# Seven products of halves for both weight products, in two stages, on one Trainium2 core

## The chip, the core and the metric

The program runs on one core of one Trainium2 chip. Five engines work on their own instruction streams and wait for each other through semaphores: TensorE (PE in the profile, with PEld its loads of the stationary operand), VectorE (DVE), ScalarE (ACT), GpSimd (POOL) and SyncE (SP), which issues nearly all DMAs. The metric is the device time of one execution in microseconds.

## The reference

```python
rms = np.sqrt(np.mean(x * x, axis=-1, keepdims=True) + 1e-06)      # q and k, each row of 64
q_n, k_n = (rmsnorm(q, g_q), rmsnorm(k, g_k))
scores = scale * np.matmul(q_n, k_n.transpose(0, 1, 3, 2))
attn = np.exp(scores - np.max(scores, axis=-1, keepdims=True))
attn = attn / (np.sum(attn, axis=-1, keepdims=True) + 1e-09)
x = np.matmul(attn, v)              # then (B,H,S,D) -> (B*S, H*D)
h = x @ w_in
g = h * (1.0 / (1.0 + np.exp(-h)))
return (g @ w_out).astype(np.float32)
```

There are 8 batches of 12 heads, 448 positions and 64 features, so x is 3584 x 768; w_in is 768 x 2048, w_out 2048 x 768. The weights come as float64 and are rounded on the chip to float32; everything is computed in float32.

## The kernel before

`bounded` (L268) is the function that runs. It takes the heads in 48 pairs, n = 0 to 47, six pairs a batch. For a pair, `normalise` (L281) squares q and k on ScalarE, reduces on VectorE, and takes the power and the two products on GpSimd; `transpose` (L309) turns q and k on TensorE, and ScalarE or VectorE copies the result out of PSUM; `scores` (L325) makes four blocks of scores and ScalarE their exponentials (L336); `weigh` (L338) multiplies them with v; `add_up` (L353) sums the exponentials on VectorE for the denominator; `divide` (L372) spreads the sums over the partitions with a matmul against ones (L379), takes the reciprocal (L383) and writes xT, a 128 x 448 tile of x transposed.

Six such tiles hold a batch. `feed_forward(b)` (L390 on) is a generator that yields after every matmul: 16 blocks f of 128 hidden features, each the sum of six matmuls of 448 columns (L400), with the activation on ScalarE out of PSUM (L408); then the product with w_out, in tiles of 128 tokens and two halves of 384 columns, 16 matmuls each (L416), copied out by VectorE (L422) and stored. A batch has 448 = 3.5 x 128 tokens, so the half tile of two batches is put together in g_joint. The hidden activations never leave the chip.

The order of everything is written out by hand: instructions stand on each engine in the order in which the program calls them. `begin` starts the feed-forward of batch b - 1 during batch b, and `fill()` (L437) is called four times a pair and emits as many matmuls as are due, evenly over the pairs. Batch 0 has nothing to fill with, and the feed-forward of batch 7 follows after the last pair. All matmuls of the feed-forward share two PSUM banks (`mm`, bufs=2).

The weights stay in SBUF. `Weights.load` (L80) brings a piece in as int64 on the SP queue, `split` (L96) takes it apart on ScalarE, `round` (L116) finishes it with three VectorE instructions and a GpSimd addition (L134 to L145). There are 24 pieces of w_in and 32 of w_out; six are rounded in batch 0 and fifty in batch 1:

```python
rounds = [0, 0, 0, 1] if b == 0 else [2, 3, 2, 3]
```

Lines of the trace name tiles: sc scores, e exponentials, es their sums, av the product with v, tr transposes and the spread sums, mm the feed-forward.

## Time and profile before

| what | value |
|---|---|
| time, median of 3 runs (lowest, highest) | 1670.94 us (1665.33, 1671.11) |
| time of the profiled execution | 1668.44 us |
| its span | 1666.6 us |
| mean granted TensorE clock | 0.986 |
| DMA traffic | 70.22 MB |
| matmuls of w_in, L400 | 1536 instructions, 604.3 us busy |
| matmuls of w_out, L416 | 1536 + 256 instructions, 517.9 + 86.8 us busy |

A float32 matmul of the program shows as two MATMUL and two LDWEIGHTS instructions. In the page's list of groups a row reads: line, engine, operation, output<-inputs, shapes, count | busy us, mean ns of one | idle time of the engine ahead of it and what ended it. In a timeline a row reads: start us, length us, engine, line, operation, and in brackets the idle time before it with its releaser.

### The profile page before, as it was taken

The numbers are of one execution on the slowest core, as the hardware profiler recorded it, in microseconds if no ns is written. First come the engines' busy times: TensorE is split into PE (matmuls) and PEld (weight loads), VectorE is DVE, ScalarE is ACT, GpSimd is POOL, SyncE is SP. The second block draws the span as 40 slices with busy tenths as digits, with TensorE's granted clock in tenths as the row PEclk, the third lists the DMA queues.
The fourth block names the chain that finished last, engine by engine and source line by source line (L and its number), as shares of the span: only waits on it lengthen the run. The fifth ranks groups of instructions, "written<-read, shape, count | busy, mean of one in ns | idle before, by whom it ended". The sixth has DMA issues, their size and how long they took to land.

```text
span 1666.6 us, 14205 instructions
## 1 busy us (share of the span) xinstructions
PE 1599.6 (96%) x5440; PEld 789.0 (47%) x5440; DVE 561.4 (34%) x660; ACT 516.9 (31%) x840; POOL 307.0 (18%) x208
## 2 busy tenths in 40 slices
PE   5887797999999999999999999999999999999998
PEld 1233343444555444544455444554455444555555
DVE  4898556422224223322322232242222422320000
ACT  4565544233212343133311343223321234211100
POOL 4555334111111121121111211211121112100000
PEclk9899999999999999999999999999999999999999
DMA  6352344100111000110011100110001100000000
GB/s 205 93 152 69 100 111 124 43 17 22 26 31 42 22 18 26 28 53 17 6 36 31 49 17 6 48 42 23 17 26 31 42 23 17 11 15 5 1 19 20
DMA packets 51984, 70.22 MB, mean 42 GB/s; under 512 B 5316, under 2 KB 44740, under 8 KB 51908
## 3 DMA queue, kind: packets, MB, share of 16 engines
q1 hardware_dynamic: 51584, 69.23, 14.5%
q8 instruction: 45, 0.74, 0.2%
q14 instruction: 31, 0.25, 0.0%
q10 hardware_dynamic: 324, 0.00, 0.0%
HBM read 58.20 MB, written 11.01 MB: 42 GB/s over the span
## 4 chain that ended last, share of the span: by engine, by line
PE 83%; DVE 2%; issue 1%; POOL 1%; ACT 1%; POOLq 0%
PE mm L416 33%; PE mm L400 32%; PE sc L331 8%; PE av L345 7%; PE tr L379 2%; PE tr L317 2%; POOL W L145 0%; DVE r L383 0%; DVE W L141 0%; DVE es L363 0%; DVE W L137 0%; DVE W L134 0%; ACT W L113 0%; ACT last L112 0%; DVE es L358 0%
## 5 line engine op out<-in xcount | busy, mean ns | idle before, releaser
L400 PE MATMUL mm<-xT,W 128*128 128x448 f32 x1536 | 604.3, 547 | 22.1 <-ACT g_joint L408 18.4
L416 PE MATMUL mm<-W,g_own 128*128 128x384 f32 x1536 | 517.9, 493 | 9.3 <-POOL W L145 6.9
L400 PEld LDWEIGHTS mm<-xT,W 128*128 128x128 f32 x1536 | 285.8, 191 | 322.6 <-issue 299.0
L416 PEld LDWEIGHTS mm<-W,g_own 128*128 128x128 f32 x1536 | 288.2, 191 | 231.2 <-issue 34.9
L297 POOL TENSOR_TENSOR rms<-rms,minus_half 112x16 f32<-112x16 f32 x48 | 139.9, 2914 | 1044.0 <-DVE rms L294 1043.4
L336 ACT ACTIVATE e<-sc 112x896 f32<-112x896 f32 x192 | 166.0, 914 | 392.6 <-PE sc L331 392.3
L383 DVE RECIPROCAL r<-tr 128x448 f32<-128x448 f32 x48 | 141.9, 2957 | 315.6 <-PE tr L379 315.6
L331 PE MATMUL sc<-qT,kT 64*112 64x448 f32 x768 | 175.4, 577 | 13.9 <-DVE kT L323 13.9
L422 DVE COPY o<-mm 128x384 f32<-128x384 f32 x56 | 31.2, 558 | 412.0 <-PE mm L416 407.3
L345 PE MATMUL av<-e,v 112*64 112x448 f32 x768 | 165.4, 552 | 0.8 <-ACT e L336 0.8
L323 DVE TENSOR_SCALAR kT<-tr,gains 128x448 f32<-128x448 f32 x48 | 32.8, 683 | 304.8 <-PE tr L317 304.8
L408 ACT ACTIVATE g_own<-mm 128x384 f32<-128x384 f32 x128 | 62.6, 489 | 199.5 <-PE mm L400 198.6
L331 PEld LDWEIGHTS sc<-qT,kT 64*112 64x112 f32 x768 | 62.7, 177 | 115.1 <-issue 84.4
L363 DVE TENSOR_TENSOR es<-es,e 112x896 f32<-112x896 f32 x96 | 108.7, 1133 | 11.4 <-ACT e L336 2.9
L345 PEld LDWEIGHTS av<-e,v 112*64 112x64 f32 x768 | 51.3, 138 | 78.7 <-issue 60.7
L416 PE MATMUL mm<-W,g_joint 128*128 128x384 f32 x256 | 86.8, 490 | 0.0
L291 ACT ACTIVATE kn<-k 112x512 f32<-112x512 f32 x48 | 30.2, 630 | 166.5 <-issue 155.6
L321 ACT COPY qT<-tr 128x448 f32<-128x448 f32 x48 | 25.6, 533 | 146.1 <-PE tr L317 146.1
L336 ACT ACT_TABLE_LOAD x43 | 55.2, 1283 | 35.5 <-PE sc L331 34.8
L416 PEld LDWEIGHTS mm<-W,g_joint 128*128 128x128 f32 x256 | 47.7, 190 | 37.3 <-issue 7.6
L408 ACT ACT_TABLE_LOAD x44 | 56.5, 1283 | 0.8
L358 DVE TENSOR_TENSOR es<-e 112x896 f32<-112x896 f32 x48 | 54.2, 1129 | 3.0 <-ACT e L336 3.0
(38 smaller groups left out, 691.0 us busy)
## 6 DMA issues: line engine op xcount, KB each, us to landing
W<-in_moe_w_in_dram SPq DMA_DIRECT2D x24, 512.0 KB, 5.1
raw<-in_moe_w_out_dram SPq DMA_DIRECT2D x32, 384.0 KB, 3.2
q<-in_q_dram SPq DMA_DIRECT2D x48, 224.0 KB, 3.2
k<-in_k_dram SPq DMA_DIRECT2D x48, 224.0 KB, 3.6
v<-in_v_dram SPq DMA_DIRECT2D x48, 224.0 KB, 3.3
out_dram<-o SPq DMA_DIRECT2D x16, 168.0 KB, 2.1
out_dram<-o SPq DMA_DIRECT2D x16, 144.0 KB, 2.1
out_dram<-o SPq DMA_DIRECT2D x16, 120.0 KB, 2.0
```

The source lines that it names most:

```text
L297: nc.gpsimd.tensor_tensor(out=flat, in0=flat, in1=minus_half[0:R].to_broadcast([R, 4 * J]), op=ALU.pow)
L317: nc.tensor.transpose(t[:, ts(j, R)], rows[:, j, :], ident[0:R, 0:R])
L331: nc.tensor.matmul(banks[:, h, 0:S], st["kT"][r, ts(j, R)], st["qT"][r, :], start=True, stop=True,)
L336: nc.scalar.activation(st["e", j], banks[:, :, 0:S], AF.Exp)
L345: nc.tensor.matmul(st["av"][ds(h * D, D), :], st["v"][:, h, j, :], st["e", j][:, h, :], start=(j == 0), stop=(j == J - 1),)
L358: nc.vector.tensor_tensor(out=st["es"], in0=st["e", 0], in1=st["e", 1], op=ALU.add)
L363: nc.vector.tensor_tensor(out=st["es"], in0=st["es"], in1=st["e", j], op=ALU.add)
L379: nc.tensor.matmul(t[ds(h * D, D), :], ones[0:R, :], st["es"][:, h, :], start=True, stop=True)
L383: nc.vector.reciprocal(out=r, in_=t)
L400: nc.tensor.matmul(h, W1[:, c, ts(f, P)], xT[b][c], start=(c == 0), stop=(c == z.NW - 1))
L408: nc.scalar.activation(dst, h[:, cols], AF.Silu)
L416: nc.tensor.matmul(t, g[:, f, :], W2[:, f, ts(half, z.HALF)], start=(f == 0), stop=(f == z.NF - 1),)
```

## The change

Both weight products are made from seven products of halves instead of eight. The left factor is split in four (a11 to a22), the right one too (b11 to b22), six sums are formed ahead, seven products run, and their results are combined while they leave PSUM:

```diff
+    def left_sums(a11, a12, a21, a22, s1, s2, s4):
+        plus(a21, a22, s1)
+        minus(s1, a11, s2)
+        minus(a11, a21, a21)
+        minus(a12, s2, s4)
+    def right_sums(b11, b12, b21, b22, t1, t2, t4):
+        minus(b12, b11, t1)
+        minus(b22, t1, t2)
+        minus(b22, b12, b12)
+        minus(b21, t2, t4)
+    def bank(n):
+        return ps.tile([P, BANK], F32, name="mm", bufs=2)[:, 0:n]
+    def seven(left, right, steps, n, done):
+        def product(name):
+            t = bank(n)
+            for i, s in enumerate(steps):
+                nc.tensor.matmul(
+                    t, left(name, s), right(name, s), start=i == 0, stop=i == len(steps) - 1
+                )
+                yield n
+            return t
+        p1, u2, u3, p5 = (parts[:, ds(i * S, n)] for i in range(4))
+        nc.scalar.copy(p1, (yield from product("1")))
+        plus((yield from product("2")), p1, done[1, 1])
+        plus((yield from product("6")), p1, u2)
+        nc.scalar.copy(p5, (yield from product("5")))
+        plus((yield from product("7")), u2, u3)
+        nc.gpsimd.tensor_tensor(out=u2, in0=u2, in1=p5, op=ALU.add)
+        nc.gpsimd.tensor_tensor(out=done[2, 2], in0=u3, in1=p5, op=ALU.add)
+        plus((yield from product("3")), u2, done[1, 2])
+        plus((yield from product("4")), u3, done[2, 1])
```

`plus` and `minus` are VectorE additions and subtractions. The two weight products no longer run together. In stage one, attention is filled with w_in alone, and the activated hidden features go to a DRAM tensor `hidden`; in stage two, w_out is multiplied alone, from tiles of 256 tokens fetched back.

Stage one: batch 0 is multiplied as before, whole (`whole`), from batch 1 on. Then the sums of the weights are formed in place (`sum_w_in`, four chunks, in batch 2), so every later batch goes by seven products: batch 1 alone in halves of 224 columns (`halves_in([1])`), both spread over batches 1 to 3; then batches 2 and 3 together with 448 columns during batches 4 and 5, 4 and 5 during 6 and 7, and 6 and 7 after the last pair. A block m of `halves_in` has seven products of three matmuls. The sums of x (`sum_x`) are formed by VectorE when two batches are complete.

```diff
+    def halves_in(group, beside=lambda m: iter(())):
+        n = len(group) * S // 2
+        for m in range(HF):
+            sum_w_in(2 * m // room.CHUNK)
...
+            for columns in seven(lambda name, c: lefts[name](c), right, range(HW), n, done):
+                count += 1
+                if count % HW == 0:
+                    next(aside, None)
+                yield columns
+            for _ in aside:
+                pass
+            for i in range(2):
+                nc.scalar.activation(rows[i], rows[i], AF.Silu)
+                save(2 * m + i, group[0] * S, rows[i])
+    def prepare_out(m):
+        if m == 0:
+            fetch(0)
+        for _ in range(room.CHUNK):
+            rounder.open()
+            yield
+            rounder.round()
+            for _ in range(NRAW - 1):
+                if rounder.loaded < rounder.rounded + NRAW:
+                    rounder.load()
+        if m % 2:
+            right_sums(*chunk_out(ORDER[m // 2]))
+        yield
+    def fetch(t):
...
+        nc.sync.dma_start(
+            dst, hidden[:, :, ds(t * 2 * P, 2 * P)].rearrange("f p c -> p f c")
+        )
+    def halves_out(t):
...
+        left_sums(a11, a12, a21, a22, s[:, 0], s[:, 1], s[:, 2])
...
+        yield from seven(lambda name, m: lefts[name][:, m], right, steps, z.HALF, done)
+        for i in range(2):
+            store(nc, out, z, (2 * t + i) * P, o[i], 0)
```

`prepare_out` rounds w_out (32 pieces, a ring of three raw buffers) beside the products of the last two batches, into the room of w_in's used chunks. `open` is the former `split`, and `Rounder` and `Room` hold the buffers. The main loop:

```diff
-        rounds = [0, 0, 0, 1] if b == 0 else [2, 3, 2, 3]
+        ends = b % 2 == 1 and b > 1 and hp == z.NPAIR - 1
...
+            if b == 1 and hp == 0:
+                begin(
+                    first_two(),
+                    z.NF * z.NW * S + products * S // 2,
+                    4 * 3 * z.NPAIR - 4,
+                )
+            elif b >= 4 and b % 2 == 0 and hp == 0:
+                sum_x([b - 2, b - 1], HW - 1)
+                begin(halves_in([b - 2, b - 1]), products * S, 4 * 2 * z.NPAIR - 4)
...
+        if b == 1:
+            room.w_in.round(room.NRAW)
+            room.w_in.open()
...
+        if b == 2 and hp in (0, 1, 2, 4):
+            sum_w_in(min(hp, room.NC - 1))
...
+        if ends:
+            finish()
+            for c in range(HW - 1):
+                sum_x([b - 1, b], c)
...
+    for _ in halves_in(group, prepare_out):
+        pass
+    fetch(1)
+    for t in range(NT // 2):
+        for _ in halves_out(t):
+            pass
+        fetch(t + 2)
```

The lines with `round` and `open` stand twice in a pair of batch 1, and once more at the end of each pair of batches 0 and 1. `work` now holds q, k, exponentials, sums and reciprocals in one tile, `stage` the hidden rows on their way to DRAM, `parts` the partial results of seven products, `x` the tiles of x.

On TensorE, a pair late in the attention stood like this before:

```order
L331 MATMUL sc<-qT,kT 112x448 x4
L416 MATMUL mm<-W_82,g_own 128x384 x10
L379 MATMUL tr<-es,ones 64x448 x2
L345 MATMUL av<-e,v_64 64x448 x4
L331 MATMUL sc<-qT,kT 112x448 x4
L416 MATMUL mm<-W_82,g_own 128x384 x11
L317 MATMUL tr<-ident,qn 128x112 x4
L345 MATMUL av<-e,v_64 64x448 x4
L416 MATMUL mm<-W_82,g_own 128x384 x10
L317 MATMUL tr<-ident,kn 128x112 x4
L416 MATMUL mm<-W_82,g_own 128x384 x10
```

And a pair of batches 4 to 7 stands like this now:

```order
L365 MATMUL sc<-work 112x448 x4
L434 MATMUL mm<-sums_x,W 128x448 x2
L434 MATMUL mm<-x_126,W 128x448 x2
L398 MATMUL tr<-work,ones 64x448 x2
L377 MATMUL av<-work,rows 64x448 x4
L365 MATMUL sc<-work 112x448 x4
L434 MATMUL mm<-x_126,W 128x448 x4
L354 MATMUL tr<-ident,work 128x112 x4
L377 MATMUL av<-work,rows 64x448 x4
L434 MATMUL mm<-sums_x,W 128x448 x3
L354 MATMUL tr<-ident,work 128x112 x4
L434 MATMUL mm<-x_126,W 128x448 x4
```

Attention stands in the same order; each stretch between its parts has three or four matmuls of 448 columns in place of ten or eleven of 384.

On VectorE, in the same place (one pair from reciprocal to reciprocal), before:

```order
L383 RECIPROCAL r<-tr 128x448
L385 TENSOR_TENSOR xT<-xU,r 128x448
L358 TENSOR_TENSOR es<-e 112x896
L422 COPY o<-mm 128x384
L363 TENSOR_TENSOR es<-es,e 112x896 x2
L323 TENSOR_SCALAR kT<-tr,gains 128x448
L292 TENSOR_REDUCE rms<-qn 112x8
L292 TENSOR_REDUCE rms<-kn 112x8
L294 TENSOR_SCALAR rms<-rms 112x16
L422 COPY o<-mm 128x384 x2
```

and now, with the rows from L408 that empty a bank:

```order
L399 RECIPROCAL work<-tr 128x448
L400 TENSOR_TENSOR x_126<-work 128x448
L388 TENSOR_TENSOR work<-work 112x896
L408 TENSOR_TENSOR stage<-mm,parts 128x448
L388 TENSOR_TENSOR work<-work 112x896 x2
L358 TENSOR_SCALAR work<-tr,gains 128x448
L330 TENSOR_REDUCE rms<-work 112x8 x2
L332 TENSOR_SCALAR rms<-rms 112x16
L408 TENSOR_TENSOR stage<-mm,parts 128x448
L408 TENSOR_TENSOR parts<-mm,parts 128x448
```

An eviction now stands behind the small work of the next pair's normalisation (L330, L332) or behind the sums (L388), and it is what two banks of three matmuls wait for. GpSimd's additions for the combination stand behind the power (L335) and the two products (L340) wherever a block's fifth product ends in a pair's last stretch.

On SP, where attention ends and the last two batches' products begin, it is now (no such work stood there before):

```order
L206 DMA rows<-in_q_dram 112x2x256
L206 DMA rows<-in_k_dram 112x2x256
L206 DMA rows<-in_v_dram 112x2x256
L460 DMA hidden<-stage 128x896 x4
L605 DMA work<-hidden 128x16x256
L63 DMA rows<-in_moe_w_out_dram 128x384 x7
```

and on ScalarE at the same place:

```order
L542 ACTIVATE stage<-stage 128x896 x2
L391 COPY work<-av 128x448
L77 ACTIVATE rows<-rows 128x384
L78 ACTIVATE x_126<-rows 128x384
L441 COPY parts<-mm 128x448
L77 ACTIVATE rows<-rows 128x384
```

The first fetch of a 2 MB tile stands ahead of the first raw piece of w_out on SP, and the opening of that piece (L77, L78) ahead of the copy that empties the first product's bank (L441) on ScalarE.

480 lines of the change are left out of this document (284 added, 196 removed).

## The prediction

> **What bounds the kernel now.** I read the page's busy shares first, then stretches of the span (columns: length, then busy time of PE, PEld, DVE, ACT and POOL with instruction counts, PE clock, DMA share, GB/s), then the chain that ended last.
>
> ```profile
> span 1666.6 us, 14205 instructions
> PE 1599.6 (96%) x5440; PEld 789.0 (47%) x5440; DVE 561.4 (34%) x660; ACT 516.9 (31%) x840; POOL 307.0 (18%) x208
> 90.87:292.00 201.13, 169.82 (x547) 79.38 (x547) 143.04 (x204) 106.73 (x187) 90.52 (x69) 0.92 0.38 110
> 292.00:1506.00 1214.00, 1214.00 (x4179) 602.18 (x4179) 346.50 (x370) 355.68 (x554) 172.87 (x105) 1.00 0.10 27
> ```
>
> From 292 us to 1506 us TensorE is never idle and its granted clock is 1.00, while VectorE is busy 29% of the time. There, time is matmul time and nothing else. Before 292 us TensorE has gaps and a clock of 0.92. So matmuls that are taken out come off the span one for one, as long as no other engine becomes late.
>
> The price of a matmul comes from the end of the chain, where attention is over (start, length, work):
>
> ```profile
> 1506.00 72.46 PE mm L400 x192
> 1578.46 82.58 PE mm L416 x256
> 1661.06 0.56 DVE o L422
> ```
>
> A float32 matmul of the program is two instructions here. 448 columns cost 72.46/192 x 2 = 0.755 us, 384 columns 82.58/256 x 2 = 0.645 us. After the last matmul (1661.04 us) 5.6 us remain to the end of the span.
>
> One head pair late in the attention shows what attention itself costs TensorE:
>
> ```profile
> 1441.81 1.69 PE sc L331 x8
> 1443.50 6.00 PE mm L416 x18
> 1449.50 0.90 PE tr L379 x4
> 1450.40 1.50 PE av L345 x8
> 1451.91 1.69 PE sc L331 x8
> 1453.60 6.00 PE mm L416 x18
> 1459.60 0.38 PE tr L317 x4
> 1459.98 1.66 PE av L345 x8
> 1461.64 6.00 PE mm L416 x18
> 1467.64 0.38 PE tr L317 x4
> 1468.03 5.82 PE mm L416 x18
> 1473.85 1.31 PE sc L331 x5
> ```
>
> The pair lasts 1473.85 - 1441.81 = 32.04 us with 72 instructions of 384 columns, 36 matmuls or 23.2 us by the price above. Attention is the other 8.8 us. Each of its four filler stretches lasts about 6 us, and that is what hides softmax, divide and transposes.
>
> **Batch 0 shows attention without filler.**
>
> ```profile
> 41.84 3.24 PE L331 MATMUL sc<-qT,kT 64*112 64x448 f32 x8 [2.43 <-DVE kT L323]
> 47.41 1.76 PE L331 MATMUL sc<-qT,kT 64*112 64x448 f32 x8
> 54.13 2.42 PE L331 MATMUL sc<-qT,kT 64*112 64x448 f32 x8 [2.24 <-DVE kT L323]
> 90.87 1.76 PE L331 MATMUL sc<-qT,kT 64*112 64x448 f32 x8 [2.07 <-DVE kT L323]
> ```
>
> The first and third row start two pairs: 54.13 - 41.84 = 12.3 us, 3.5 us above 8.8. TensorE waits for kT, which VectorE makes late. After a gap of 2.43 us the same scores take 3.24 instead of 1.76 us: a gap also costs clock, 1.5 us here. Batch 1 starts at 90.9 us.
>
> **A floor for the old kernel:** 90.9 + 42 pairs x 8.8 (369.6) + 768 x 0.755 (579.8) + 896 x 0.645 (577.9) + 5.6 = 1623.8 us. The span has 42.8 us more. Since nothing waits after 292 us, these lie in batch 1, where 50 weight pieces are rounded beside the filler.
>
> **The change, part by part.**
>
> *Matmuls removed.* w_in: 96 of 448 columns for batch 0, 168 of 224 for batch 1 (worth 84), 3 x 168 for the other six: 684 instead of 768. That is 84 x 0.755 = 63.4 us. w_out: 14 tiles x 7 products x 8 = 784 instead of 896, 112 x 0.645 = 72.2 us. Together 135.6 us. The floor becomes 1623.8 - 135.6 = 1488.2 us: start 91, batches 1 to 3 294, batches 4 to 7 465, w_in of the last two 127, w_out 506, end 6. All else is waits against this floor.
>
> *Additions added.* Durations of the nearest rows (mean ns after the comma):
>
> ```profile
> L383 DVE RECIPROCAL r<-tr 128x448 f32<-128x448 f32 x48 | 141.9, 2957 | 315.6 <-PE tr L379 315.6
> L363 DVE TENSOR_TENSOR es<-es,e 112x896 f32<-112x896 f32 x96 | 108.7, 1133 | 11.4 <-ACT e L336 2.9
> L323 DVE TENSOR_SCALAR kT<-tr,gains 128x448 f32<-128x448 f32 x48 | 32.8, 683 | 304.8 <-PE tr L317 304.8
> L297 POOL TENSOR_TENSOR rms<-rms,minus_half 112x16 f32<-112x16 f32 x48 | 139.9, 2914 | 1044.0 <-DVE rms L294 1043.4
> L145 POOL TENSOR_TENSOR W<-W,last 128x384 int32<-128x384 int32 x32 | 34.1, 1072 | 61.8 <-DVE W L141 49.2 <-ACT W L113 10.1 <-ACT g_joint L408 1.6
> L302 POOL TENSOR_TENSOR qn<-q,rms 112x512 f32<-112x512 f32 x48 | 51.2, 1067 | 3.8
> ```
>
> A block of seven products has five VectorE additions out of PSUM (0.68 us by the kT row, which also reads 448 columns of PSUM), two GpSimd additions (1.07 us for 384, so about 1.25 us for 448) and two ScalarE copies. A pair of batches 4 to 7 holds 0.73 block, so VectorE gains 2.4 us on some 9.5 us of attention work, in a pair of 8.8 + 10.6 = 19.4 us on TensorE. It fits; the question is the order.
>
> *Batches 4 to 7.* A filler stretch shrinks from 6 us to 1710 columns, 2.9 us. Going through one pair by these rows: the longest thing ahead of an eviction is reciprocal and multiply (about 3.6 us) after the first stretch, beside ones, av and scores (4.1 us) on TensorE. The tight place is the last stretch: after the k transposes come kT 0.68, two reduces of 0.68 and a small one of 0.17, so an eviction that stands behind them is done 3 us after the transposes, while TensorE asks for its bank after 2.3 to 2.9 us. I take 0.7 us a pair, 17 us in all. The lower bound is 0; the upper is that every pair waits as in batch 0, 24 x 3.5 = 84 us. Where product 7 ends in the last stretch, its GpSimd additions stand behind the power and two multiplies (2.9 + 1.07 + 1.07), and the eviction of product 3 waits for them; with one block in four so placed, and most of it covered by the scores, this is inside the 0.7.
>
> *Batches 1 to 3.* Stretches are 1186 columns, 2.0 us. Batch 1 rounds 18 pieces instead of 50: 42.8 x 18/50 = 15 us (bounds 0 and 42.8). Batch 2 adds 16 sums of 768 elements of the weights, about 1 us each by the es row, four in a row ahead of kT in four pairs: half of it hidden, 8 us (0 to 16). Batch 1's own products have 224 columns and last 3 x 0.377 = 1.1 us, so the two banks cover only that; I take two waits of 1 us in each of its 8.4 pairs, 17 us (0 to 40). Sum 40 us.
>
> *Boundaries.* At the ends of batches 3 and 5 about one pair has no filler, like batch 0: 2 x 4 = 8 us (0 to 20).
>
> *w_in of the last two batches, with w_out rounded beside it.* The first raw w_out load is queued on SP behind the fetch of the first 2 MB tile, and ScalarE waits for it ahead of the copy of product 1, so TensorE stops after two products (4.5 us).
>
> ```profile
> W<-in_moe_w_in_dram SPq DMA_DIRECT2D x24, 512.0 KB, 5.1
> q<-in_q_dram SPq DMA_DIRECT2D x48, 224.0 KB, 3.2
> GB/s 205 93 152 69 100 111 124 43 17 22 26 31 42 22 18 26 28 53 17 6 36 31 49 17 6 48 42 23 17 26 31 42 23 17 11 15 5 1 19 20
> DMA packets 51984, 70.22 MB, mean 42 GB/s; under 512 B 5316, under 2 KB 44740, under 8 KB 51908
> ```
>
> By the first two rows 2 MB take 20 us (4 x 5.1) to 29 us (9.4 x 3.2) if time grows with size; at the 205 GB/s of the span's first slice, where loads stand in the queue as they do here, 10 us. I take 10, plus 3.2 for the raw load, less 4.5 of products and about 3 us (the last reciprocal) by which the fetch is issued ahead: 6 us, bounds 0 and 25. To this comes 1 us for each of eight blocks, where ScalarE opens four pieces besides its copies (0 to 3 each). Sum 14 us (0 to 49).
>
> *w_out alone.* A product is 8 x 0.645 = 5.2 us and a bank has that long; four sums of 1024 elements are about 5 us on VectorE, once in a tile of 36 us, and are wanted only by the third product. A fetch of even 29 us fits in a tile. 3 us (0 to 10).
>
> *DRAM traffic* grows by 59 MB (16 x 128 x 3584 x 4 bytes, written and read). Batch 1 ran at 110 GB/s by the stretch above; 70 + 59 = 129 MB in 1570 us is 82 GB/s. Nothing is added for it.
>
> **Sum.** Waits 17 + 40 + 8 + 14 + 3 = 82; 1488.2 + 82 = 1570 us of span. The profiled run took 1668.44 us for its span of 1666.6, so 1.8 more: **1572 us**. That run is 2.5 us under the median of the three, well inside 0.5%, which is about what a measurement of this kernel can tell from no change.
>
> **A rule that speaks against it.** The rows of batch 0 give 1.5 us of lost clock after a gap of 2.43 us and none after 2.07. The Trainium skill, "TensorE: Matmul & The Clock Gate", section "A second HAM failure mode: psum-queue depth-cycling", says that short idles between groups of matmuls that cycle through PSUM banks can make the clock swing between half and full. Its section "What's actually happening" puts the window at about 3.4 us; the trace loses clock after less. By that rule groups of three matmuls on two banks would be worse than the groups of 6 and 16, which the trace has run at 1.00, and the time would be that of rival (a); by the rows alone the sum stays as it is.
>
> **Rivals.** (a) *The clock.* The attention's part of the floor from batch 1 on is 294 + 465 = 759 us. At the 0.92 of the stretch with gaps it would be 825: 66 us more, 1638. For: that stretch. Against: from 292 us on, the same attention code keeps 1.00, and gaps below 2.1 us cost nothing. (b) *Batch 0 everywhere.* Every pair waits 3.5 us for kT: 42 x 3.5 = 147 in place of 65: 1654. For: shorter stretches. Against: batch 0 had no filler at all, and here four stretches of 2 to 2.9 us stand in the same places. (c) *Slower:* VectorE and GpSimd hold each other. An eviction waits for a GpSimd addition behind the power, 2.9 + 2.1 + 1.25 = 6.3 us, and all of VectorE's queue behind it: reciprocal, kT, the next eviction. If that comes on top of (b) in every one of the 24 blocks, it is 147 + 24 x 6.3 (151) = 298: 1488 + 298 + 17 + 2 = 1805. It decides from 1668.4 x 1.005 - 1490 = 187 us of waits, less 17 behind attention: 4.0 us a pair. Against: only one block in four has its additions there. (d) *The halves don't pay in batch 1:* at 224 columns the weight load is as long as the matmul, so if it weren't hidden, 336 loads would be added:
>
> ```profile
> L400 PEld LDWEIGHTS mm<-xT,W 128*128 128x128 f32 x1536 | 285.8, 191 | 322.6 <-issue 299.0
> ```
>
> 336 x 0.19 = 64 us: 1636. Against: the loads of 0.19 us vanish beside the matmuls in the pair above. (e) *Waits stay small,* as after 292 us: 82 becomes 25, 1515.
>
> **How the numbers follow.** Forecast (1535 to 1615) 0.62; (e) 0.14; (a) 0.07; (d) 0.03; (b) 0.08; (c) 0.06. The range 1505 to 1645 holds the first four and leaves out (b) and (c), 0.14, with a little of the rest. Faster by over 0.5% (under 1662): all but (c) and a part of (b), 0.90; within 0.5%: that part of (b), 0.04; slower: 0.06.
>
> **What would show it.** In the changed profile the w_out part should be 506 to 516 us with TensorE solid at 1.00, and w_in of the last two batches 127 to 176 us with one gap near its start, ended by ScalarE's opening of the first piece. Pairs of batches 4 to 7 should take 19.4 to 21 us on average (12 pairs in 235 to 250 us); 23 us would be (b), a clock under 0.95 there (a). Waits of matmuls for evictions should be named "DVE stage" or "DVE parts" and stay near 1 us each; waits of VectorE for POOL of 5 us and more would be (c). The prediction is wrong if w_out's stage has gaps between tiles (a late fetch), or if attention's pairs are bound by VectorE.

## The result, and the profile after

The changed kernel takes **1548.4 us** (median of 4 runs, 1545.57 to 1553.14) against 1668.4 us before (median of 4), a ratio of **0.928 with a 95% interval of 0.925 to 0.932**. The forecast was 1572 us, in a range of 1505 to 1645: faster, as foretold, and by 24 us more than foretold. The profiled run took 1545.57 us for a span of 1543.8 us.

The span and the busy shares from the page of the changed kernel:

```profile
span 1543.8 us, 14413 instructions
PE 1464.2 (95%) x5216; PEld 743.5 (48%) x5216; DVE 759.0 (49%) x970; ACT 525.3 (34%) x744; POOL 408.7 (26%) x300
```

TensorE has 135.4 us less work (1599.6 before), VectorE 198 us more, GpSimd 102 us more, and the traffic is the 129 MB of the sum (128.96 MB on the page). TensorE is still busy 95% of the time, so the time is still matmuls plus what TensorE waits.

The same kernel by stages, in stretches of the span (length, then busy time of PE, PEld, DVE, ACT, POOL, the granted clock, DMA share and GB/s). Batch 0 lies ahead of them, up to 90.67 us; the four are batches 1 to 3, batches 4 to 7, w_in of the last two batches, and w_out:

```profile
90.67:412.79 322.12, 300.30 (x1320) 156.47 (x1321) 223.25 (x288) 199.52 (x271) 128.02 (x89) 0.99 0.27 82
412.79:889.46 476.67, 469.07 (x1725) 202.60 (x1725) 273.73 (x320) 215.39 (x282) 157.61 (x101) 0.99 0.19 62
889.46:1031.73 142.27, 130.10 (x339) 64.57 (x337) 93.33 (x162) 50.90 (x95) 51.91 (x48) 0.98 0.47 150
1031.73:1537.60 505.87, 505.84 (x1569) 297.73 (x1567) 103.87 (x126) 14.85 (x30) 27.21 (x28) 1.00 0.25 77
```

Set against the terms of the prediction (floor plus waits):

| stage | floor | waits foretold | measured length | over the floor |
|---|---|---|---|---|
| start to batch 1 | 91 | 0 | 90.7 | 0 |
| batches 1 to 3, and the boundary after 3 | 294 | 40 + 4 | 322.1 | 28 |
| batches 4 to 7, and the boundary after 5 | 465 | 17 + 4 | 476.7 | 12 |
| w_in of the last two | 127 | 14 | 142.3 | 15 |
| w_out | 506 | 3 | 505.9 | 0 |
| end | 6 | 0 | 6.2 | 0 |

82 us of waits were foretold, and 55.6 came (the span less the floor of 1488.2 us). The floor itself is shown best where nothing waits: w_out took 505.9 us for its 506. An eviction, in what follows, is the instruction that reads a full bank out of PSUM and so frees it for the next product. Where TensorE waited, from the view of waits (waiting instruction, releaser, us in total, times, longest):

```profile
PE sc L365 <- DVE work L358: 17.8, 10, 3.5
PE mm L434 <- DVE stage L408: 15.6, 13, 2.0
PE tr L354 <- POOL work L340: 15.1, 1, 15.1
PE mm L434 <- DVE parts L408: 9.3, 4, 2.3
PE mm L434 <- ACT parts L441: 2.8, 1, 2.8
```

The third and 15.1 us of the first lie in the start and batch 0, which both kernels share. The seven products brought the other three: evictions to `stage` and `parts`, and the first eviction of the last two batches.

**Batch 1's blocks.** The products of 224 columns waited 15.5 us, nearly the 17 us foretold. Of these, 13.9 us were for VectorE's evictions and 1.6 us for ScalarE's last activation of batch 0 (view of waits between 190 and 420 us):

```profile
PE mm L434 <- DVE stage L408: 13.9, 9, 2.0
PE mm L434 <- ACT stage L472: 1.6, 1, 1.6
```

For most of the 13.9 us the timeline names a cause that the prediction had given only to its slower rival. TensorE, VectorE and GpSimd in one pair of batch 3 (start, length, work, and the idle time before it with its releaser), first TensorE:

```profile
308.85 1.76 PE L365 MATMUL sc<-work 64*112 64x448 f32 x8
310.54 1.40 PE L434 MATMUL mm<-x,W 128*128 128x224 f32 x6
313.59 1.02 PE L434 MATMUL mm<-x,W 128*128 128x224 f32 x4 [1.65 <-DVE stage L408]
```

VectorE:

```profile
302.38 0.17 DVE L332 TENSOR_SCALAR rms<-rms 112x16 f32<-112x16 f32 x1
302.47 0.38 DVE L408 TENSOR_TENSOR parts<-mm,parts 128x224 f32<-128x224 f32 x1
308.31 0.39 DVE L408 TENSOR_TENSOR stage<-mm,parts 128x224 f32<-128x224 f32 x1 [5.46 <-POOL parts L446]
308.62 2.95 DVE L399 RECIPROCAL work<-tr 128x448 f32<-128x448 f32 x1
311.60 0.62 DVE L400 TENSOR_TENSOR x<-work 128x448 f32<-128x448 f32 x1
312.15 1.08 DVE L388 TENSOR_TENSOR work<-work 112x896 f32<-112x896 f32 x1
313.15 0.38 DVE L408 TENSOR_TENSOR stage<-mm,parts 128x224 f32<-128x224 f32 x1
```

GpSimd:

```profile
302.64 2.90 POOL L335 TENSOR_TENSOR rms<-rms,minus_half 112x16 f32<-112x16 f32 x1 [12.43 <-DVE rms L332]
305.62 2.04 POOL L340 TENSOR_TENSOR work<-rows,rms 112x512 f32<-112x512 f32 x2
307.62 0.66 POOL L446 TENSOR_TENSOR parts<-parts 128x224 f32<-128x224 f32 x1
```

Product 7 is evicted at 302.47, just after the sum that starts GpSimd's power. The addition of 0.66 us that product 3's eviction needs stands behind the power and two multiplies and ends at 308.3. VectorE stands for 5.46 us; then reciprocal, multiply and a sum come first, product 4 is evicted at 313.15, and TensorE, which wanted that bank, has waited 1.65 us. A block of batch 1 lasts about one pair, so the same place comes round once in every block: in each of the eight, VectorE stands 5.45 or 5.46 us there. In seven of them TensorE then waits 1.64 to 2.03 us for an eviction, 12.3 of the 13.9 us together. Another 1.32 us stand behind the last group of w_in's sums, which VectorE ends at 280.38 us, just ahead of an eviction.

**The last two batches.** VectorE in the second block of that stage:

```profile
921.71 0.95 DVE L405 TENSOR_TENSOR x<-x 128x768 f32<-128x768 f32 x1
923.56 2.70 DVE L405 TENSOR_TENSOR x<-x 128x768 f32<-128x768 f32 x3 [0.90 <-POOL x L111]
926.17 0.62 DVE L408 TENSOR_TENSOR parts<-mm,parts 128x448 f32<-128x448 f32 x1
```

Four sums for w_out stand ahead of product 7's eviction, and the second waits for GpSimd to round the last piece. TensorE stops 2.33 us for that eviction, in each of the four odd blocks: the 9.3 us above.

### The profile page after: what moved, and what is told of

It is laid out like the page before. It is cut to its first block, busy times and chain, and to the rows that moved or that the text cites. A ratio compares the mean times of both kernels' runs of the same rounds, so it can differ in the third digit from the quotient of the medians.

```text
span 1543.8 us, 14413 instructions
## 1 busy us (share of the span) xinstructions
PE 1464.2 (95%) x5216; PEld 743.5 (48%) x5216; DVE 759.0 (49%) x970; ACT 525.3 (34%) x744; POOL 408.7 (26%) x300
## 2 busy tenths in 40 slices
DMA packets 87924, 128.96 MB, mean 84 GB/s; under 512 B 5924, under 2 KB 70948, under 8 KB 87844
## 5 line engine op out<-in xcount | busy, mean ns | idle before, releaser
L434 PE MATMUL mm<-x,W 128*128 128x448 f32 (+1 forms) x768 | 283.4, 507 | 14.7 <-DVE stage L408 13.1
L335 POOL TENSOR_TENSOR rms<-rms,minus_half 112x16 f32<-112x16 f32 x48 | 141.0, 2937 | 408.4 <-DVE rms L332 394.9
L368 ACT ACTIVATE work<-sc 112x896 f32<-112x896 f32 x192 | 166.1, 914 | 203.3 <-PE sc L365 203.0
L434 PE MATMUL mm<-sums_x,W 128*128 128x448 f32 (+1 forms) x576 | 210.9, 500 | 14.7 <-DVE parts L408 9.3
L434 PEld LDWEIGHTS mm<-x,W 128*128 128x128 f32 x768 | 141.1, 192 | 148.6 <-issue 122.8
L434 PE MATMUL mm<-W,work 128*128 128x384 f32 x588 | 197.6, 486 | 0.0
L365 PE MATMUL sc<-work 64*112 64x448 f32 x768 | 175.4, 577 | 17.8 <-DVE work L358 17.8
L399 DVE RECIPROCAL work<-tr 128x448 f32<-128x448 f32 x48 | 141.8, 2953 | 88.7 <-PE tr L398 88.7
L408 DVE TENSOR_TENSOR stage<-mm,parts 128x448 f32<-128x448 f32 (+2 forms) x121 | 67.7, 562 | 237.5 <-PE mm L434 101.2
L408 DVE TENSOR_TENSOR parts<-mm,parts 128x448 f32<-128x448 f32 (+2 forms) x92 | 51.6, 561 | 265.7 <-PE mm L434 256.5
L388 DVE TENSOR_TENSOR work<-work 112x896 f32<-112x896 f32 x144 | 169.0, 1174 | 12.1 <-ACT work L368 5.5
L377 PE MATMUL av<-work,rows 112*64 112x448 f32 x768 | 165.3, 552 | 3.6 <-ACT work L368 3.6
L441 ACT COPY parts<-mm 128x448 f32<-128x448 f32 (+2 forms) x46 | 21.8, 474 | 268.9 <-PE mm L434 268.9
L434 PE MATMUL mm<-W,x 128*128 128x384 f32 x336 | 112.9, 486 | 0.0
L340 POOL TENSOR_TENSOR work<-rows,rms 112x512 f32<-112x512 f32 x96 | 100.6, 1069 | 3.8
```

Source lines behind the costliest of these rows:

```text
L335: nc.gpsimd.tensor_tensor(out=flat, in0=flat, in1=minus_half[0:R].to_broadcast([R, 4 * J]), op=ALU.pow)
L340: nc.gpsimd.tensor_tensor(out=normal[name].rearrange("p j h d -> p h j d"), in0=st[name], in1=factor.to_broadcast([R, 2, J, D]), op=ALU.mult,)
L365: nc.tensor.matmul(banks[:, h, 0:S], kT[rows, ts(j, R)], qT[rows, :], start=True, stop=True)
L368: nc.scalar.activation(e[j], banks[:, :, 0:S], AF.Exp)
L377: nc.tensor.matmul(st["av"][ds(h * D, D), :], st["v"][:, h, j, :], e[j][:, h, :], start=(j == 0), stop=(j == J - 1),)
L388: nc.vector.tensor_tensor(out=es, in0=e[0] if j == 1 else es, in1=e[j], op=ALU.add)
```

## The experiments

All runs go against the kernel before on the same chip; the median is given first. For stages I use the lengths from each run's profile.

### The changed kernel again

> The changed kernel once more, unaltered, as the measure for the three runs beside it. Every theory expects its 1548 us again, within about 4 us, with a span made up as in its first profile: some 322 us from the start of batch 1 to the start of batch 4, 477 us for batches 4 to 7, 142 us for w_in of the last two batches, 506 us for w_out.

1548.59 us (0.928, 0.927 to 0.929): the measure for what follows. Its stages are 323.9, 475.4, 146.2 and 505.8 us.

### Whose fault are batch 1's waits: GpSimd's additions on VectorE

```diff
-        nc.gpsimd.tensor_tensor(out=u2, in0=u2, in1=p5, op=ALU.add)
-        nc.gpsimd.tensor_tensor(out=done[2, 2], in0=u3, in1=p5, op=ALU.add)
+        plus(u2, p5, u2)
+        plus(u3, p5, done[2, 2])
```

> The two GpSimd additions of each block of seven products are done by VectorE instead; nothing is left out. In the profile of the changed kernel TensorE waits 15.5 us for VectorE's evictions of batch 1's products of 224 columns. Theory A (they come from GpSimd's queue: in each of these blocks VectorE stood 5.46 us for an addition that stood behind the power, and everything behind it came late): those waits fall to under 4 us and the time by about 12 us, to 1536. Theory B (what the prediction gave as their cause: two banks cover only a product's 1.1 us, so any eviction that is a little late stops TensorE): VectorE only has 2 x 0.62 us more in each block, the waits stay at 13 us or more, and the time is 1547 to 1553 us.

1534.60 us, 14.0 less: theory A. Waits and batches 1 to 3 of this run:

```profile
PE mm L434 <- DVE stage L408: 6.0, 12, 1.3
```

```profile
90.46:399.67 309.21, 299.27 (x1320) 155.28 (x1320) 228.71 (x304) 198.46 (x271) 117.75 (x73) 0.99 0.28 85
```

The waits fell from 15.6 to 6.0 us (in batches 1 to 3 from 13.9 to 4.1, just missing the 4 that theory A gave) although VectorE has more to do in each block. (The expectation puts all 15.5 us on VectorE's evictions; the 1.6 us that were ScalarE's are still there.) The stage is 12.9 us shorter than in the first profile, and TensorE is idle for 9.9 us of it instead of 21.8. So most of these waits came from GpSimd's queue. Two banks were cover enough once it was out of the way, except for 4.1 us; what a third bank would have done with the additions left on GpSimd no run shows.

### Batch 1 whole

```diff
         yield from whole(0)
-        for c in range(HW):
-            sum_x([1], c)
-        yield from halves_in([1])
+        yield from whole(1)
...
-                    z.NF * z.NW * S + products * S // 2,
+                    2 * z.NF * z.NW * S,
...
-        if b == 2 and hp in (0, 1, 2, 4):
-            sum_w_in(min(hp, room.NC - 1))
+        if b == 3 and hp in (0, 2, 4):
+            sum_w_in(hp // 2)
```

> Batch 1 is multiplied whole (96 matmuls of 448 columns) instead of by seven products of 224 columns (168 of half the length, worth 84); w_in's sums come in batch 3 instead of batch 2; nothing is left out. 12 x 0.755 = 9.1 us of matmul time more. Theory A (the waits of the 224-column blocks cost more than these blocks save): the 14 us that adds_dve gained go here too, 1548.5 + 9.1 - 14 = 1543.6 us, a little under the changed kernel. Theory B (the waits are of batch 1 to 3's short stretches, whatever is in them, or of w_in's sums): 1552 to 1558 us.

1532.20 us (0.918, 0.917 to 0.919): 16.4 less, though TensorE has 9.1 us more to do; even better than theory A. Its batches 1 to 3:

```profile
90.15:396.77 306.62, 304.78 (x1176) 129.24 (x1176) 201.75 (x232) 202.63 (x261) 117.70 (x73) 0.99 0.28 86
```

That is 303.1 (294 + 9.1) plus 3.5. TensorE is idle for 1.8 us of it, nearly all of that ahead of batch 4's first scores. The rounding is the same, the stretches are nearly as short (1265 columns for 1186), and three of the four groups of w_in sums stand in batch 3 instead of batch 2. In the changed kernel only the last of these groups has a wait behind it, the 1.32 us above, so moving them explains little. Two waits for exponentials in batch 1 (1.06 and 1.53 us), ahead of any block, went as well; why isn't shown. So the blocks of 224 columns brought most of the waits, and in batch 1 they cost more than they saved.

### w_out's sums behind the last eviction

```diff
             ...
-        if m % 2:
-            right_sums(*chunk_out(ORDER[m // 2]))
         yield
+        yield
+        yield
+        if m % 2:
+            right_sums(*chunk_out(ORDER[m // 2]))
```

> In w_in of the last two batches the four VectorE sums of each w_out chunk (L405, 768 elements) are issued behind the block's last eviction instead of ahead of product 7's; nothing is left out. Theory A: the four gaps of 2.33 us there come from product 7's eviction standing behind these sums and behind the GpSimd addition that they wait for; behind the last eviction they have a product of 2.26 us evicted by ScalarE and one of their own to hide beside, so the gaps go and the time falls by 9.3 us, to 1539; the stage takes 133 us instead of 142.3. Theory B: the sums of 3.8 us have no room in a block in which VectorE also rounds four pieces, and the gap only moves to the next block's first VectorE eviction: 1546 to 1549 us.

1538.30 us, 10.3 less: theory A. No wait for "DVE parts" is left, and the stage takes 134.8 us:

```profile
894.10:1028.90 134.80, 130.34 (x338) 65.50 (x337) 91.78 (x159) 51.24 (x95) 49.55 (x48) 0.97 0.50 159
```

### An earlier start of the last two batches: a miss

```diff
-        if m == 0:
+        if m == 4:
             fetch(0)
...
-    divide(last)
     group = [z.B - 2, z.B - 1]
+    finish()
+    for _ in range(NRAW):
+        rounder.load()
+    rest = halves_in(group, prepare_out)
+    for _ in range(HW):
+        next(rest)
+    divide(last)
     sum_x(group, HW - 1)
-    for _ in halves_in(group, prepare_out):
+    for _ in rest:
         pass
```

> Three edits at the start of w_in of the last two batches, nothing left out: the first three raw w_out loads are issued ahead of the last divide, the fetch of the first 2 MB tile is issued with the fifth block instead of the first, and the first product (which needs batch 6 alone) is issued ahead of the last divide's ones-matmuls. Theory A: TensorE's wait of 2.39 us for the last sum of exponentials is covered by the product, the clock that was lost behind it (0.5 from 887.5 to 894.3 us, 3.4 us lost) stays, and the wait of 2.82 us for ScalarE's opening of the first piece goes since the load no longer stands behind the fetch: 2.4 + 3.4 + 2.8 = 8.6 us, 1540. Theory B (the fetch isn't what the load waited for, ScalarE's own queue is): only the first two terms or less, 1543 to 1548, and a wait for ScalarE's opening is still there.

1549.70 us, 1.1 more than the changed kernel: nothing gained, against both theories. TensorE in this run, at the start of the stage:

```profile
889.26 2.52 PE L434 MATMUL mm<-x,W 128*128 128x448 f32 x6
894.00 2.51 PE L434 MATMUL mm<-sums_x,W 128*128 128x448 f32 x4 [2.22 <-ACT parts L441]
897.60 1.86 PE L434 MATMUL mm<-sums_x,W 128*128 128x448 f32 x2 [1.08 <-DVE sums_x L405]
900.46 4.83 PE L434 MATMUL mm<-sums_x,W 128*128 128x448 f32 x6 [1.00 <-DVE stage L408]
```

The wait of 2.39 us ahead of the last divide is gone, and the first products run at once. But VectorE, here from its first sum behind the last sum of exponentials to the eviction that ends TensorE's third wait, is no sooner done:

```profile
888.13 0.62 DVE L405 TENSOR_TENSOR sums_x<-x 128x448 f32<-128x448 f32 x1
...
892.66 2.95 DVE L399 RECIPROCAL work<-tr 128x448 f32<-128x448 f32 x1
...
897.99 0.62 DVE L405 TENSOR_TENSOR sums_x<-x,sums_x 128x448 f32<-128x448 f32 x1
...
899.78 0.62 DVE L408 TENSOR_TENSOR stage<-mm,parts 128x448 f32<-128x448 f32 x1
```

Twelve sums of 0.62 us, the last reciprocal and its multiply keep it busy without a break until 898.5 us, then the rounding of the first piece, which now comes early, stands ahead of product 2's eviction. Three short waits took the place of two here, a fourth of 2.16 us came up in the fifth block, behind the moved fetch, and the clock fell further:

```profile
894.00:906.00 12.00, 9.91 (x15) 3.97 (x16) 11.62 (x19) 3.24 (x7) 2.99 (x3) 0.57 0.27 73
```

Hiding one wait uncovered the next engine. That VectorE is the limit there is read from the trace; no run took its sums away.

### Each weight product undone

w_out by eight plain products, without its sums:

```diff
-        left_sums(a11, a12, a21, a22, s[:, 0], s[:, 1], s[:, 2])
...
-        yield from seven(lambda name, m: lefts[name][:, m], right, steps, z.HALF, done)
+        for i, j in done:
+            t_ = bank(z.HALF)
+            count = 0
+            for m in steps:
+                for k in (1, 2):
+                    nc.tensor.matmul(
+                        t_, lefts[i, k][:, m], right((k, j), m),
+                        start=count == 0, stop=count == 2 * HF - 1,
+                    )
...
```

> The w_out stage alone is undone: eight plain products for each two tiles of 128 tokens (4 results of 16 matmuls), without the sums of the hidden rows and of w_out; w_in keeps the seven products. 112 matmuls of 384 columns more. Theory A (matmuls come off one for one): the stage grows by 112 x 0.645 = 72.2 us to 578 us, and the four gaps of 2.33 us that w_out's sums made in the stage before go (late_sums: 10.3 us): 1548.5 + 72.2 - 10.3 = 1610 us. Theory B (the seven products paid less than their matmuls, in waits or clock inside the stage): the stage is under 570 us and the time under 1603.

1610.06 us: theory A to the microsecond. The stage, with its predecessor:

```profile
889.30:1023.70 134.40, 129.88 (x338) 65.42 (x338) 79.01 (x146) 51.47 (x95) 49.71 (x48) 0.97 0.50 159
1023.70:1601.80 578.10, 578.05 (x1793) 341.01 (x1791) 15.70 (x29) 14.34 (x29) 0.00 (x0) 1.00 0.22 68
```

578.1 - 505.9 = 72.2 us, exactly the matmuls removed. The stage before it is 8 us shorter than in the first profile: the four gaps of w_out's sums are gone, and its first wait is 4.5 us instead of 2.8. In all, undoing w_out costs 61.5 us (1548.59 to 1610.06), since its sums cost the stage ahead of it some 10 us.

w_in by plain products: `whole` in place of `halves_in` for every batch, without its sums.

```diff
-                sum_x([b - 2, b - 1], HW - 1)
-                begin(halves_in([b - 2, b - 1]), products * S, 4 * 2 * z.NPAIR - 4)
+                begin(two(b - 2), 2 * z.NF * z.NW * S, 4 * 2 * z.NPAIR - 4)
...
-    for _ in halves_in(group, prepare_out):
-        pass
+    count = 0
+    for _ in two(group[0]):
+        if count % (4 * z.NW) == 0:
+            aside = prepare_out(count // (4 * z.NW))
+        count += 1
+        if count % HW == 0:
+            next(aside, None)
```

> w_in alone is undone: every batch is multiplied whole, by 96 matmuls of 448 columns each, ScalarE's Silu reads PSUM, and there are no sums of w_in and of x and no evictions by VectorE and GpSimd in that stage; w_out keeps the seven products in its own stage. 84 matmuls worth 448 columns more, 63.4 us. Theory A (one for one, and the waits that the seven products brought go with them): the 14 us that adds_dve gained and some 10 us of the last two batches' 12.2 us of gaps go (VectorE's evictions, not its sums, are what TensorE waited for): 1548.5 + 63.4 - 24 = 1588 us. Theory B (the waits belong to the shorter stretches and to rounding, not to the seven products): 1548.5 + 63.4 = 1612 us.

1565.02 us, where the theories said 1588 and 1612: the seven products of w_in bring even less than theory A left them. Here and in `both_plain` below, w_out's pieces overwrite parts of w_in that batch 7 still reads, so its hidden rows are of other weights. It was therefore run once more with the last two batches in turns:

```diff
-    def whole(b):
+    def whole(*bs):
...
         for f in range(z.NF):
-            h = bank(S)
...
+            for b in bs:
+                h = bank(S)
...
-    for _ in two(group[0]):
+    for _ in whole(*group):
```

> w_in by plain products as in win_plain, with batches 6 and 7 multiplied in turns, block by block, so that w_in stays whole until both have used it (in win_plain and both_plain w_out's pieces took the place of w_in's under batch 7, so batch 7's hidden rows were of other weights there, with the same instructions). Theory A (the data don't matter for the time): 1565 us within 3. Theory B (the missing order made those two runs shorter): 1575 us or more.

1562.74 us (0.937, 0.935 to 0.938): theory A, so the order did not make the time. Its stages:

```profile
89.64:396.27 306.63, 304.81 (x1176) 129.34 (x1176) 191.26 (x220) 202.45 (x261) 117.70 (x73) 0.99 0.28 86
396.27:900.40 504.13, 500.04 (x1820) 220.35 (x1820) 210.48 (x212) 264.74 (x327) 113.53 (x69) 1.00 0.19 59
900.40:1047.40 147.00, 146.35 (x386) 73.60 (x385) 72.60 (x118) 47.59 (x96) 34.26 (x32) 0.99 0.47 147
```

Against the changed kernel: batches 1 to 3 15.5 us shorter, batches 4 to 7 27.5 longer, the last two 4.7 longer. TensorE has 63.4 us more to do, and the time grows by 14 to 16 us. With ScalarE's Silu reading the banks, TensorE hardly waits at all: it is idle for 1.8, 4.1 and 0.7 us of the three stages.

Both undone (the edits of `win_plain` and `wout_plain`), so that only the staging of the change is left:

> Only the staging of the change is kept: attention with w_in, hidden rows to DRAM, then w_out alone with its weights rounded in between, but both products plain, with the matmuls of before (135.6 us more than now). It tells what the seven products bring and what the staging brings. Theory A (the staging itself gains: 18 instead of 50 pieces are rounded beside batch 1, whose waits were 42.8 us; the trip through DRAM is hidden): 1548.5 + 135.6 - 24 - 10 = 1650 us, 1 percent under before. Theory B (the staging is neutral or costs, the stretches of 3.6 us instead of 6 us and the trip through DRAM give back what rounding no longer takes): 1668 us or more.

1636.63 us (0.980, 0.979 to 0.982): theory A, and a gain 13 us larger than it foretold. With exactly the matmuls of before, the staging alone takes 33.5 us off the 1670.1 us that the kernel before took beside it. Batches 1 to 3 last 306.6 us, as in `win_whole`, 3.2 over their floor (18 x 8.8 + 192 x 0.755 = 303.4): the 42.8 us of waits of before are nearly gone. Which part of the staging does this, fewer pieces to round or w_in alone as filler, no run separates.

Together these runs split the gain of about 120 us: **33.5 us staging, 71.6 us w_out** (1636.63 to 1565.02), **some 16 us w_in** (1565.02 to 1548.59; 14 from `win_whole`). The split holds for this order. With w_in's seven products kept, w_out is worth 61.5 us, and with w_out plain, w_in is worth 26.6 us (1636.63 to 1610.06). The two share some 10 us: w_out's sums stand in VectorE's queue ahead of w_in's evictions, which is what `late_sums` took away.

### How much room has VectorE: each eviction twice

```diff
+    def evict(t, other, out):
+        for _ in range(2):
+            plus(t, other, out)
...
-        plus((yield from product("2")), p1, done[1, 1])
+        evict((yield from product("2")), p1, done[1, 1])
...
```

(and so for products 6, 7, 3 and 4)

> Each of VectorE's five evictions in a block of seven products is done twice, with the same result; nothing is left out. It adds 5 x 0.62 = 3.1 us of VectorE time to a block (2.3 us to a pair of batches 4 to 7, whose VectorE is busy 108.6 of 202.1 us between 673 and 875 us). Theory A (VectorE has room between its deadlines in batches 4 to 7, and only the blocks of batch 1 and the odd blocks of the last two batches, where it is already late, pass the time on): pairs of batches 4 to 7 stay under 20.6 us on average, all in all 1553 to 1563 us. Theory B (the tight last stretch of the prediction: an eviction stands 0.7 us late there, so each 0.62 us more is waited for): 0.6 us and more for each of 24 pairs, average pairs over 20.9 us, and 1570 us or more.

1581.45 us: the total that theory B gave, and far above theory A's. The stages say where it came:

```profile
90.08:428.15 338.07, 310.46 (x1320) 160.42 (x1320) 237.73 (x328) 199.64 (x271) 127.69 (x89) 0.96 0.26 78
428.15:910.00 481.85, 467.94 (x1725) 201.62 (x1725) 323.13 (x398) 215.96 (x282) 157.65 (x101) 1.00 0.19 61
910.00:1065.90 155.90, 137.21 (x338) 67.14 (x338) 115.15 (x203) 51.35 (x95) 51.94 (x48) 0.94 0.43 137
```

Batches 4 to 7 take 481.9 us, 20.1 a pair, for 49 us more of VectorE work (323.1 against 273.7): 5 to 6 us more, not the 20.9 a pair of theory B. There theory A holds, and the tight place of theory B isn't found: its total came for another reason. The other 24 to 30 us lie where VectorE was late already, in batches 1 to 3 with batch 1's blocks (14 to 16) and in the last two batches (10 to 14). What theory A had too small was the price of lateness there, where each longer wait also took clock (0.96 and 0.94 in those stretches).

### Is the trip through DRAM hidden: three fetches for one

```diff
-        nc.sync.dma_start(
-            dst, hidden[:, :, ds(t * 2 * P, 2 * P)].rearrange("f p c -> p f c")
-        )
+        for _ in range(3 if t else 1):
+            nc.sync.dma_start(
+                dst, hidden[:, :, ds(t * 2 * P, 2 * P)].rearrange("f p c -> p f c")
+            )
```

> In the w_out stage each 2 MB tile of hidden rows but the first is fetched three times to the same place, with the same result; nothing is left out. 13 tiles x 4 MB = 54 MB more through the DMA engines beside the stage's 506 us. Theory A (the trip through DRAM is hidden: a fetch lands in 9 us and has a tile's 36 us): three take 27 us and still fit, the stage stays at 506 us and the time at 1546 to 1551 us. Theory B (the stage has little cover left, or the stores of the output wait behind the fetches): the stage grows by 5 us or more, the time to 1554 or more.

1548.28 us: theory A. The stage at 185 GB/s instead of 77, with TensorE as solid as before:

```profile
1034.40:1540.20 505.80, 505.80 (x1569) 297.72 (x1567) 103.86 (x126) 14.86 (x30) 27.23 (x28) 1.00 0.59 185
```

### The causes mended together

The edits of `b1_whole`, `adds_dve` and `late_sums`, and `fetch(0)` with the fifth block.

> Four edits of the changed kernel together, nothing left out: batch 1 whole (b1_whole), the two GpSimd additions on VectorE (adds_dve), w_out's sums behind the block's last eviction (late_sums), and the fetch of the first tile issued with the fifth block, so that the first raw w_out loads don't stand behind it. Theory A (three separate causes): b1_whole's 1532.2, less the 10.3 us of late_sums, less 1 to 3 us for the first piece; the additions have little left to gain once batch 1 has no blocks: 1519 to 1522 us. Theory B (the gains overlap or VectorE, with more to do in each block of the last two batches, gives one back): 1526 us or more.

**1522.70 us, 0.912 of before (0.911 to 0.913)**: 26 us under the changed kernel, and the best time of the study. It is nearest to theory A, 0.7 us above its upper end: the late fetch only moved the wait for a raw load to the block that it now stands in, where ScalarE waits 8.06 us for it, and TensorE behind ScalarE (view of waits):

```profile
PE mm L434 <- ACT parts L444: 3.0, 1, 3.0
```

The four edits were made at once, so what each gives here is read from the total: 1532.2 less 10.3 is 1521.9, which leaves nothing for the moved additions and the late fetch. The plain batch 1 and the moved additions mend the same waits, so their gains of 16.4 and 14.0 us don't add up; that of the sums does.

## Why the prediction was right, point by point

**The matmuls came off one for one: right, and shown.** In w_out 72.2 us foretold, 72.2 measured in the stage when undone. TensorE's work fell by 135.4 us (135.6 in the sum), and the prices of 0.755 and 0.645 us held: w_out took 505.9 us for the floor's 506.

**The waits were mis-sized, 82 for 55.6 us.** This is the whole error of 24 us and more: on the same floor the sum would have been 1546 with the measured waits. No term that was too small hid one that was too large; luck lies inside the terms, in two that had the right size and the wrong cause. Term by term:

- *Batches 1 to 3, 40 us and 4 of a boundary; measured 28.* The step that failed worst is "Batch 1 rounds 18 pieces instead of 50: 42.8 x 18/50 = 15 us". The waits did not scale with the number of pieces: up to 196 us, while the 18 pieces are rounded, TensorE has three gaps in the changed kernel, 3.8 us together, and where the products are plain, the pieces and everything else leave 3.2 us over the floor. "Half of it hidden, 8 us" for w_in's sums was too much as well: three of their four groups in batch 3 of `b1_whole` leave TensorE without a gap, and in the changed kernel one of four has a wait behind it, of 1.32 us.
- *The 17 us for products of 224 columns: right in size (15.5) by luck, wrong in cause.* "The two banks cover only that" was the reason given. The runs showed GpSimd's queue: with the additions moved away the waits fell by 9.6 us and the time by 14, with the same banks and columns. In all, the blocks cost 25.5 us over their matmuls (the 16.4 us that `b1_whole` gained and its 9.1 us of matmuls), of which 11.5 us remain with the additions moved.
- *Batches 4 to 7, 0.7 us a pair and a boundary, 21 us; measured 12,* of which TensorE is idle for 7.6 us. Pairs took 476.7/24 = 19.9 us (19.4 to 21 foretold). The tight last stretch has room: 2 us more of eviction to a pair cost 0.2 us.
- *The last two batches, 14 us; measured 15, in another place.* That the totals agree is luck. The wait for the first load, 6 us in the sum, was 2.8 us in the first profile, but 4.4 us in `again` and 3.8 to 6.3 us in the six other runs whose stage starts the same way, so this term was not far off. The "1 us for each of eight blocks", put down to ScalarE, were four gaps of 2.33 us, made by VectorE's sums ahead of an eviction, which the sum had not looked at.
- *w_out, 3 us: none.* A fetch landed in 9 us where 10 was taken, and three of them still fit. (The 9.4 in the bound of the fetch should be 2048/224 = 9.1; its 29 us are by that.)

Why the waits of batch 1 went can be read from the kernel before, where they stood in a few places (view of waits from 80 to 340 us):

```profile
PE mm L400 <- ACT g_joint L408: 18.4, 3, 9.9
```

At 162.73, 204.99 and 249.78 us ScalarE had stood 8.34, 6.18 and 6.17 us for GpSimd's last addition to a piece (L145) before it could open the next. The two longest of the three waits in that row, 7.04 and 9.92 us, ended behind the first two of these: the activation that empties TensorE's bank stood behind the opening on ScalarE. In the changed kernel's batch 1, ScalarE stands no more than 1.8 us for that addition.

**Rivals.** (a), a clock of 0.92 in attention, didn't come: 0.99 in both stretches of attention behind batch 0. The argument against it, that gaps below 2.1 us cost nothing, came from one row and was wrong, as the last section shows. What the Trainium skill says in "TensorE: Matmul & The Clock Gate", section "A second HAM failure mode: psum-queue depth-cycling", of a clock that swings with such groups, there of bf16 and 512 columns, isn't borne out: from 673 to 875 us groups of three matmuls of 448 columns in float32 ran on two banks at a granted clock of 1.00, with TensorE idle for 0.9 us. (b) is out, with pairs of 19.9 us. (d) is out too: once GpSimd's queue no longer held these blocks up, batches 1 to 3 took 309.2 us with their 168 matmuls of 224 columns (`adds_dve`) and 306.6 with 96 of 448 in their place (`b1_whole`). TensorE was busy 3.6 us longer with them than the price of their columns asks (299.27 for 304.78 - 9.1), which leaves little to the loads, and not 64 us. (e), waits of 25 us in all, didn't come either: 55.6 us lie between it and the 82 of the forecast. (c) is the instructive one. Its mechanism was there: thirteen times VectorE stood 4.6 to 5.7 us for GpSimd, in each of batch 1's eight blocks among them. The prediction's test for it ("waits of VectorE for POOL of 5 us and more would be (c)") would have said slower. In seven of batch 1's eight blocks it cost TensorE 1.6 to 2.0 us instead of 6.3, since, by the timeline above, VectorE's delay first used up the cover of two banks, the scores and the weighing. A test by VectorE's wait alone was the wrong test; it must be TensorE's wait behind it.

**What the prediction gave the wrong credit.** It put the waits that batch 1 loses at 42.8 - 15 = 27.8 us, as one term among others. The staging alone brought 33.5 us, twice what w_in's 63.4 us of saved matmuls brought in the end.

## What to carry to other kernels

Matmuls taken out of a stage in which TensorE never waits are gained in full; taken out of a stage that other engines share, they shorten the cover of everything else there, so look first for instructions that stand in one in-order queue ahead of an eviction (a power on GpSimd, a group of sums on VectorE) and move those. Undo each part of a change by itself even when the whole is a gain: here one part (batch 1 by halves) was a loss of 16 us inside a gain of 120, and w_out's part was 71.6 or 61.5 us by whether w_in's was there. When a wait is taken away, ask which engine is next late at the same place: the early start of the last two batches gained nothing.

## What the hardware showed that was not expected

Short gaps can cost more than their length, and not evenly. After the gap of 2.39 us that ended at 887.76 us the granted clock was half for some 7 us, while six gaps of 0.3 to 1.65 us that ended between 255 and 321 us cost none. Two stretches of the changed kernel:

```profile
887.70:894.50 6.80, 6.74 (x11) 2.81 (x12) 6.73 (x9) 0.17 (x1) 0.00 (x0) 0.52 1.04 339
255.00:321.00 66.00, 59.05 (x299) 38.78 (x300) 41.93 (x62) 33.05 (x49) 18.53 (x15) 1.00 0.22 67
```

The length of a gap doesn't decide it. Two gaps of the same length in the changed kernel, each ahead of a product of 224 columns:

```profile
370.01 1.02 PE L434 MATMUL mm<-x,W 128*128 128x224 f32 x4 [2.03 <-DVE stage L408]
389.07 2.59 PE L434 MATMUL mm<-x,W 128*128 128x224 f32 x6 [2.02 <-DVE stage L408]
```

Behind the first the granted clock was 1.00 (370.0 to 373.4 us), behind the second 0.52 (389.0 to 392.5 us). The gap of 2.82 us that ended at 899.44 us and the four of 2.33 us in the last two batches cost no clock at all, and in `again` the gap at the same place as that of 2.39 us, 2.40 us long, was followed by half the clock for 3.3 us and not for 6.8. In the early start, waits of 2.22, 1.08 and 1.00 us close together brought the clock to 0.57 over 12 us. So in this kernel a wait of 2.4 us can cost nearly 6 (half of 7 us on top), or only itself. The Trainium skill, "TensorE: Matmul & The Clock Gate", section "What's actually happening", tells of a free-running window of about 3.4 us; that gaps of one length differ, and that the loss came as about one or two such lengths behind a single gap, agrees with it. That the clock is lost only behind an idle window of that length does not: here gaps of 2.0 to 2.4 us were enough.
